# Averaging tile 1 by halves on two engines, and moving its sum of squares behind tile 3, at the start of a two-layer attention and feed-forward kernel

## The chip, the cores and the metric

The kernel runs on one core of one Trainium2 chip. The metric is the device time of one execution in microseconds (us). One execution per kernel was also recorded by the profiler; its span is about 1.8 us shorter than the timed value of the same execution. In the profile, PE is TensorE (matmul), PEld its weight loads, DVE is VectorE, ACT is ScalarE, POOL is GpSimd, SP is SyncE, and "SPq" or "ACTq" are the instructions with which SP and ACT issue DMAs.

## The reference, cut to what matters

```python
x = A_x                                       # 2048 tokens x 1024, bf16
x = x + _A_ref(_layernorm(x), A_wqkv, A_wo)   # sliding attention, 32 heads
x = x + _B_ref(_layernorm(x), B_w1, B_w3, B_w2)   # gated feed-forward, F = 3584
x = x + _A_ref(_layernorm(x), A_wqkv, A_wo)
x = x + _B_ref(_layernorm(x), B_w1, B_w3, B_w2)
return x
```

The layer norm subtracts the mean and divides by sqrt(var + 1e-5). The change touches only the very first layer norm and Q projection: the first 512 tokens, four tiles of 128 tokens each, called tiles 0 to 3.

## The kernel before

The kernel does not emit instructions in the order in which its text is written. It builds a list of operations with estimated durations, and a planner lays them out; the finished order is then emitted. On every engine, instructions run in that order.

```python
def place(self, n_banks=8, rate=330e3):
    # ... repeatedly takes the operation that can start first by the estimates:
    #     PE: the heads of three lanes (0 projections, 1 output projection, 2 transposes)
    #     other engines: smallest start, then class, then number
    ...
        if e in ("SP", "AQ"):                       # a DMA
            free[e] = t + op.dur                    # 0.45 us of the queue, for every DMA
            begin = max(pipe[e], t + 1.3)
            ...
    placed.sort(key=lambda o: (o.start, o.seq))
    return placed
# ... at the end of the kernel:
        for op in pr.place():
            op.emit(op)
```

The first Q projection (`q_first`) avoids waiting for a full layer norm of tiles 0 and 1. It only centres them (subtracts the mean), transposes the centred tiles on PE into `ce`, multiplies by Wq, and brings in 1/std later. The squares that give the std of tiles 0 and 1 run on ScalarE. Tiles 2 and 3 are fully normalized first (statistics, root, reciprocal, apply) and transposed on PE. The weights Wq come in eight row blocks, "row 0" to "row 7".

```python
dve(0.77, ... nc.vector.tensor_scalar(xn[2][:, 0:512], x_sb[0][:, 0:512], 1.0 / D, ..., accum_out=mean[:, 0:1]), ...)
act(0.82, ... nc.scalar.activation(xn[3][:, 0:512], x_sb[0][:, 512:1024], ..., accum_out=part[:, 0:1]), ...)
act(1.25, ... nc.scalar.activation(xn[3][:], x_sb[1][:], ..., accum_out=mean[:, 1:2]), ...)   # tile 1: all on ScalarE
for j in range(2):
    # centring of tile j in two halves on VectorE, then:
    transposed(xn[j], ..., ((0, 2, "DVE"), (2, 4, "DVE"), (4, 8, "ACT")) if j == 0 else ((0, 4, "DVE"), (4, 8, "ACT")))
...
for j in range(2, TPC):                       # tiles 2 and 3
    stats(j, ...); root(j, j + 1); apply(j); transposed(xn[j], ...)
for j in range(2):                            # squares of tiles 0 and 1, root, reciprocal, scaling
    act(1.25, ... ACTF.Square ..., accum_out=part[:, j:j + 1]), [..., ("ce", 1, KT - 1)], ...)
    ...
    dma(256, xnT[b][:, :, j * P:(j + 1) * P], xn[j][:], ..., transpose=True)     # for K and V
```

The K projection follows the Q projection; it needs all four tiles normalized and transposed in `xnT`, tiles 0 and 1 by DMA transpose. The loads of the next tokens wait for tile 1 to be normalized (`load_x(1, 0, 4, [("xn", 1)])`).

## Time and profile before

| | before |
|---|---|
| time, median of the first 3 runs | 1614.96 us (1614.86 to 1615.26) |
| span of the profiled run | 1613.1 us |
| PE busy | 1601.3 us |
| first matmul of the K projection | 21.49 us |

The page of the kernel before: busy time and share of the span with the number of instructions; PE's busy tenths in 40 slices; and, from the chain of work that ended last, the shares by engine.

```profile
PE 1601.3 (99%) x7463; PEld 762.7 (47%) x7610; DVE 1122.3 (70%) x1906; ACT 329.6 (20%) x526; POOL 5.3 (0%) x28
...
PE   9999999999999999999999999999999999999999
...
PE 99%; issue 1%; DMA 0%; ACT 0%; DVE 0%; ACTq 0%
```

The waits view of PE for the kernel before: who waited for whom, us in total, times, longest.

```profile
PE bank L285 <- PEq L757: 0.8, 1, 0.8
PE bank L430 <- DVE xn L472: 0.4, 1, 0.4
PE bank L521 <- DMA slot<-in_A_wqkv_dram: 0.2, 1, 0.2
```

So PE streams from about 7 us to the end, and nothing outside its queue is worth anything unless it makes PE wait. The timeline of the start, kernel before: start, duration, engine, line, operation, output from input, size, count, and in brackets the idle time before it and what ended it.

```profile
3.10 0.69 DVE L454 TENSOR_SCALAR_CACHE_REDUCE xn<-x 128x512 bf16<-128x512 bf16 x1 [2.10 <-DMA x<-in_A_x_dram]
...
5.37 1.06 ACT L460 ACTIVATE xn<-x 128x1024 bf16<-128x1024 bf16 x1 [1.35 <-DMA x<-in_A_x_dram]
...
6.33 0.19 ACT L460 ACTIVATION_READ_ACCUMULATOR xn<-x 128x1 f32 x1
...
6.55 0.62 DVE L472 TENSOR_SCALAR xn<-x,mean 128x512 bf16<-128x512 bf16 x2 [1.22 <-ACT xn L460]
...
6.96 0.66 PE L430 MATMUL bank<-ident,xn 128*128 128x128 bf16 x8 [0.39 <-DVE xn L472]
...
7.46 5.44 PE L521 MATMUL bank<-hT,slot 128*128 128x128 bf16 x64
...
14.51 7.15 PE L535 MATMUL bank<-xnT,slot 128*128 128x256 bf16 x64
...
21.49 8.80 PE L347 MATMUL bank<-xnT,slot 128*128 128x512 bf16 x39
```

The last line is the start of the K projection; its length and count end with the view's window. Tile 1's average (5.37 to 6.52) stands between its landing and its centring at 6.55, and PE waits 0.39 us for it. This wait is what the change is after.

### The profile page before, as it was taken

The page shows a single profiled execution, that of the slowest core. Times are in us where ns is not written, and L with a number is a line of the kernel's source. Part 1 is how long each engine was busy: PE and PEld are TensorE (multiplying, and loading weights), DVE is VectorE, ACT ScalarE, POOL GpSimd, SP SyncE. Part 2 cuts the span into 40 slices and gives each one's busy share as a digit, 9 for nine tenths or more (in the row PEclk, how much of TensorE's full clock was granted, in tenths as well). Part 3 has the DMA queues.
Part 4 walks back from the last instruction along what each step waited for, and adds up shares of the span by engine and source line. Part 5 has one row for each costly group of instructions (what it writes and reads, how often), then busy time and mean ns, then how long its engine had stood idle before and what let it go on. Part 6 is the DMA issues. An engine that isn't in the chain of part 4 may idle for free.

```text
span 1613.1 us, 19082 instructions
## 1 busy us (share of the span) xinstructions
PE 1601.3 (99%) x7463; PEld 762.7 (47%) x7610; DVE 1122.3 (70%) x1906; ACT 329.6 (20%) x526; POOL 5.3 (0%) x28
## 2 busy tenths in 40 slices
PE   9999999999999999999999999999999999999999
PEld 7555544444444444444444444444444444444444
DVE  5899888988889888898898729884299831211211
ACT  5423322021201222113311032110321101101110
POOL 1000000000000000000000000000000000000000
PEclk9999999999999999999999999999999999999999
DMA  9834755495548764858545487365873464454451
GB/s 321 228 105 151 221 166 171 127 227 158 171 141 253 194 186 137 216 164 251 176 131 163 157 248 228 121 176 174 254 220 118 160 179 156 144 177 149 156 167 42
DMA packets 350649, 285.80 MB, mean 177 GB/s; under 512 B 72288, under 2 KB 344928, under 8 KB 350560
## 3 DMA queue, kind: packets, MB, share of 16 engines
q1 hardware_dynamic: 350128, 283.94, 58.8%
q8 instruction: 59, 0.97, 0.2%
q10 hardware_dynamic: 432, 0.66, 0.1%
q14 instruction: 30, 0.25, 0.1%
HBM read 238.94 MB, written 29.36 MB: 166 GB/s over the span
## 4 chain that ended last, share of the span: by engine, by line
PE 99%; issue 1%; DMA 0%; ACT 0%; DVE 0%; ACTq 0%
PE bank L347 98%; PE bank L535 0%; PE bank L521 0%; DMA x<-in_A_x_dram 0%; PE bank L430 0%; ACT L281 0%; DVE xn L472 0%; ACT xn L460 0%; DVE x L700 0%; ACTq L460 0%
## 5 line engine op out<-in xcount | busy, mean ns | idle before, releaser
L347 PE MATMUL bank<-xnT,slot 128*128 128x512 bf16 x4955 | 1088.7, 379 | 5.3
L347 PEld LDWEIGHTS <-slot 128*128 128x128 bf16 x5056 | 518.2, 102 | 572.9
L347 PE MATMUL bank<-slot,hT 128*128 128x512 bf16 (+2 forms) x1812 | 387.3, 372 | 1.9
L670 DVE TENSOR_TENSOR hT<-sg,bank 128x512 bf16<-128x512 bf16 x224 | 153.4, 685 | 214.4 <-PE bank L347 194.9
L265 DVE TENSOR_TENSOR scr<-scr 128x1024 bf16<-128x1024 bf16 (+3 forms) x576 | 293.4, 539 | 2.0
L347 PEld LDWEIGHTS <-hT 128*128 128x128 bf16 x1848 | 178.5, 98 | 208.7
L668 ACT ACTIVATE sg<-bank 128x512 bf16<-128x512 f32 x224 | 133.7, 597 | 660.5 <-PE bank L347 608.8
L265 DVE TENSOR_TENSOR scr<-qT,kT 128x2048 bf16<-128x2048 bf16 x128 | 154.1, 1219 | 73.3 <-DMA kT<-qkv_d 71.0
L405 ACT CAST sgt<-bank 128x512 bf16<-128x512 f32 x184 | 107.3, 585 | 315.2 <-PE bank L347 300.3
L265 DVE TENSOR_TENSOR scr<-pA,vT 128x2048 bf16<-128x2048 bf16 x128 | 152.5, 1220 | 0.3
L700 DVE TENSOR_TENSOR x<-x,bank 128x512 bf16<-128x512 bf16 (+1 forms) x66 | 43.9, 670 | 121.5 <-PE bank L347 121.4
L347 PE MATMUL bank<-wo,oT 128*128 128x512 bf16 x502 | 112.6, 379 | 0.6
L313 DVE BATCH_NORM_STATS2 st<-x 128x6 f32<-128x512 bf16 x124 | 81.8, 681 | 11.9 <-DMA x<-in_A_x_dram 11.4
L347 PEld LDWEIGHTS <-oT 128*128 128x128 bf16 x512 | 50.1, 98 | 60.3
L645 DVE TENSOR_TENSOR x<-x,bank 128x512 bf16<-128x512 bf16 x64 | 43.9, 687 | 37.0 <-PE bank L347 35.8
L320 ACT ACTIVATE sd<-mv,epst 128x4 f32<-128x4 f32 (+1 forms) x17 | 5.1, 297 | 172.4 <-DVE mv L316 172.1
L628 DVE STREAM_TRANSPOSE pA<-pB 128x2048 bf16<-128x2048 bf16 x16 | 37.0, 2310 | 0.5
L605 DVE STREAM_TRANSPOSE pB<-pA 128x2048 bf16<-128x2048 bf16 x16 | 37.0, 2310 | 0.5
L668 ACT ACT_TABLE_LOAD x20 | 25.7, 1283 | 56.2 <-PE bank L347 56.0
L265 DVE TENSOR_TENSOR pA<-scr 128x256 bf16<-128x256 bf16 x128 | 35.9, 286 | 0.4
L265 DVE TENSOR_TENSOR oT<-scr 128x256 bf16<-128x256 bf16 x128 | 33.9, 288 | 0.1
L327 DVE TENSOR_SCALAR xn<-x,mv,rstd 128x1024 bf16<-128x1024 bf16 x62 | 30.7, 541 | 3.5 <-DMA xnT<-xn 3.4
(61 smaller groups left out, 209.0 us busy)
## 6 DMA issues: line engine op xcount, KB each, us to landing
slot<-in_B_w_dram SPq DMA_DIRECT2D x160, 1024.0 KB, 5.9
slot<-in_A_wqkv_dram SPq DMA_DIRECT2D x28, 1024.0 KB, 5.1
qkv_d<-sgt SPq DMA_DIRECT2D x92, 256.0 KB, 3.3
qT<-qkv_d SPq DMA_DIRECT2D x16, 512.0 KB, 5.7
slot<-in_B_w_dram SPq DMA_DIRECT2D x16, 512.0 KB, 5.7
kT<-qkv_d SPq DMA_DIRECT2D x14, 544.0 KB, 6.7
vT<-qkv_d SPq DMA_DIRECT2D x14, 544.0 KB, 4.9
out_dram<-x SPq DMA_DIRECT2D x31, 128.0 KB, 4.3
```

The lines of the kernel that those rows point to most:

```text
L265: return lambda _: nc.vector.tensor_tensor(o, a, b, op=op)
L313: dve(0.67, lambda _, hh=hh: nc.vector.bn_stats(st[q][:, j, hh, :], x_sb[n][:, hh * 512:(hh + 1) * 512]), [("x", n, hh)] + list(after), [( ...
L320: act(0.3, lambda _: nc.scalar.activation(sd[q][:, j0:j1], mv[q][:, j0:j1, 1], ACTF.Sqrt, bias=epst[:]), [("mv", q, j) for j in range(j0, ...
L327: dve(0.5, lambda _: nc.vector.tensor_scalar(xn[j][:], x_sb[n][:], mv[q][:, j, 0:1], rstd[q][:, j:j + 1], op0=ALU.subtract, op1=ALU.mult), ...
L347: nc.tensor.matmul(bank[a.bank][:, 0:ncol], lhsT=w, rhs=r, start=first and i == 0, stop=last and i == n - 1)
L405: evac(act, 0.59, lambda _, a=a, i=i, m=m: nc.scalar.copy(sgt[i][:, m % 2, :], bank[a.bank][:]), op, [], [("sgt", i, m % 2)], a)
L605: dve(2.31, lambda _: nc.vector.transpose(psmT[:].rearrange("p c d -> p (c d)"), psm[:].rearrange("p w s -> p (w s)")), allA, ["pB"])
L628: dve(2.31, lambda _: nc.vector.transpose(At[:].rearrange("p w s -> p (w s)"), AeT[:].rearrange("p c d -> p (c d)")), ["pB"], allA)
L645: evac(dve, t1(512), lambda _, xs=xs, a=a: nc.vector.tensor_tensor(xs, xs, bank[a.bank][:], op=ALU.add), op, [("x", n, hh)], [("x", n, hh) ...
L668: evac(act, 0.6, lambda _, i=i, a=ag: nc.scalar.activation(sg[i][:], bank[a.bank][:], ACTF.Silu), og, [], [("sg", i)], ag, table="silu")
L670: evac(dve, t1(512), lambda _, i=i, a=au, f=f: nc.vector.tensor_tensor(hT[:, f, :], sg[i][:], bank[a.bank][:], op=ALU.mult), ou, [("sg", i ...
L700: evac(dve, t1(cn), lambda _, xs=xs, a=a, cn=cn: nc.vector.tensor_tensor(xs, xs, bank[a.bank][:, 0:cn], op=ALU.add), op, [("x", n, hh)], [ ...
```

## The change

Tile 1 is averaged like tile 0: its left half on VectorE, its right half on ScalarE at the same time. Its centring takes the two partial means as two scalars, and its transposes are evacuated in three pieces. ScalarE's square of tile 1 moves behind the evacuation of tile 3's transposes, so that it stands in nobody's way.

```diff
-        act(1.25, lambda _: nc.scalar.activation(xn[3][:], x_sb[1][:], ACTF.Copy, scale=1.0 / D,
-                                                 accum_out=mean[:, 1:2]), [("x", 1, 0), ("x", 1, 1)], ...)
         for j in range(2):
+            dve(0.77, lambda _, j=j: nc.vector.tensor_scalar(xn[2][:, 0:512], x_sb[j][:, 0:512], ...,
+                                                             accum_out=mean[:, j:j + 1]),
+                [("x", j, 0)] + [("ce", 0, 2)] * j, [("xn", 2), ("mean", j)], -9)
+            act(0.82, lambda _, j=j: nc.scalar.activation(xn[3][:, 0:512], x_sb[j][:, 512:1024], ...,
+                                                          accum_out=part[:, j:j + 1]), ...)
 ...         # centring: mean and part as two scalars for both tiles
-                       ((0, 2, "DVE"), (2, 4, "DVE"), (4, 8, "ACT")) if j == 0 else ((0, 4, "DVE"), (4, 8, "ACT")))
+                       ((0, 2, "DVE"), (2, 4, "DVE"), (4, 8, "ACT")))
 ...         # the square:
-                [("x", j, 0), ("x", j, 1), ("mean", j)] + [("ce", 1, KT - 1)],
+                [("x", j, 0), ("x", j, 1), ("mean", j), ("xnT", b, 3, 1) if j else ("ce", 1, KT - 1)],
```

The loop also takes in tile 0's two averaging instructions, which stay as they were; their removed lines are left out here.

More of the change, by code (lines that the diff above doesn't have):

```diff
@@ L453, in q_first @@
         ce = hT[:, 8:16, :]
-        dve(0.77, lambda _: nc.vector.tensor_scalar(xn[2][:, 0:512], x_sb[0][:, 0:512], 1.0 / D, 0.0, op0=ALU.mult,
-                                                    op1=ALU.add, accum_out=mean[:, 0:1]),
-            [("x", 0, 0)], [("xn", 2), ("mean", 0)], -9)
-        act(0.82, lambda _: nc.scalar.activation(xn[3][:, 0:512], x_sb[0][:, 512:1024], ACTF.Copy, scale=1.0 / D,
-                                                 accum_out=part[:, 0:1]), [("x", 0, 1)], [("xn", 3), ("part", 0)], -9)
@@ L459, in q_first @@
-        rows[2](6, queue="AQ", after=[("part", 0)])
-        act(1.25, lambda _: nc.scalar.activation(xn[3][:], x_sb[1][:], ACTF.Copy, scale=1.0 / D,
-                                                 accum_out=mean[:, 1:2]), [("x", 1, 0), ("x", 1, 1)],
-            [("xn", 3), ("mean", 1)], -9)
-        for j in range(2):
-            for h in range(2):
-                c0 = 512 * h
-                if j == 0:
-                    dve(0.31, lambda _, c0=c0: nc.vector.tensor_scalar(
-                        xn[0][:, c0:c0 + 512], x_sb[0][:, c0:c0 + 512], mean[:, 0:1], part[:, 0:1], op0=ALU.subtract,
-                        op1=ALU.subtract), [("x", 0, 0), ("x", 0, 1), ("mean", 0), ("part", 0)],
-                        [("xn", 0), ("xn", 0, h)], -9)
-                else:
-                    dve(0.31, lambda _, c0=c0: nc.vector.tensor_scalar(
-                        xn[1][:, c0:c0 + 512], x_sb[1][:, c0:c0 + 512], mean[:, 1:2], None, op0=ALU.subtract),
-                        [("x", 1, 0), ("x", 1, 1), ("mean", 1)], [("xn", 1), ("xn", 1, h)], -9)
+        for j in range(2):
+            dve(0.77, lambda _, j=j: nc.vector.tensor_scalar(xn[2][:, 0:512], x_sb[j][:, 0:512], 1.0 / D, 0.0,
+                                                             op0=ALU.mult, op1=ALU.add, accum_out=mean[:, j:j + 1]),
+                [("x", j, 0)] + [("ce", 0, 2)] * j, [("xn", 2), ("mean", j)], -9)
+            act(0.82, lambda _, j=j: nc.scalar.activation(xn[3][:, 0:512], x_sb[j][:, 512:1024], ACTF.Copy,
+                                                          scale=1.0 / D, accum_out=part[:, j:j + 1]),
+                [("x", j, 1)], [("xn", 3), ("part", j)], -9)
+            if j == 0:
+                rows[2](6, queue="AQ", after=[("part", 0)])
+            for h in range(2):
+                dve(0.31, lambda _, j=j, c0=512 * h: nc.vector.tensor_scalar(
+                    xn[j][:, c0:c0 + 512], x_sb[j][:, c0:c0 + 512], mean[:, j:j + 1], part[:, j:j + 1],
+                    op0=ALU.subtract, op1=ALU.subtract), [("x", j, 0), ("x", j, 1), ("mean", j), ("part", j)],
+                    [("xn", j), ("xn", j, h)], -9)
@@ L475, in q_first @@
             transposed(xn[j], [("xn", j, h) for h in range(2)], ce[:, :, j * P:(j + 1) * P],
                        [("ce", j, k) for k in range(KT)],
-                       ((0, 2, "DVE"), (2, 4, "DVE"), (4, 8, "ACT")) if j == 0 else ((0, 4, "DVE"), (4, 8, "ACT")))
-        dve(0.16, lambda _: nc.vector.tensor_tensor(mean[:, 0:1], mean[:, 0:1], part[:, 0:1], op=ALU.add),
-            [("mean", 0), ("part", 0), ("ce", 1, 0)], [("mean", 0)], -9)
+                       ((0, 2, "DVE"), (2, 4, "DVE"), (4, 8, "ACT")))
@@ L480, in q_first @@
+        dve(0.16, lambda _: nc.vector.tensor_tensor(mean[:], mean[:], part[:], op=ALU.add),
+            [("mean", j) for j in range(2)] + [("part", j) for j in range(2)] + [("ce", 1, 0)],
+            [("mean", j) for j in range(2)], -9)
         for j in range(2, TPC):
```

## The prediction

> **What bounds the kernel.** TensorE. The page gives PE 1601.3 of 1613.1 us busy (99%), and the chain that ended last is 99% PE. From about 7 us to the end PE streams; the waits view of PE finds only three waits: 0.8 us at the start, 0.4 us for the centred tile 1, and 0.2 us for a weight row. The change touches only the first 22 us.
>
> **The stretch before, from the timeline.** Tile 1's data lets ScalarE start at 5.37. Its full-width average takes 5.37 to 6.52; VectorE idles 1.22 us, then centres from 6.55; the transposes of tile 1 start at 6.96. After that PE runs without a gap: matmuls from 7.46, transposes of tiles 2 and 3, the second group at 14.51, the K projection at 21.49.
>
> **Costs.** Removed: one 1024-wide ACT average (1.15 us). Added: a 512-wide half on VectorE (0.69 + 0.08, tile 0's durations) and one on ScalarE (0.63 + 0.19, overlapping to 0.72). The Trainium skill, "ScalarE: Activation LUTs", section "What ACT_TABLE_LOAD costs", gives 186 ns + 0.833 ns per element with immediates, 613 and 1039 ns; the trace shows 629 and 1057, so it agrees. Both halves end near 6.10, not 6.52: 0.42 us sooner. The centring with two scalars costs 0.41 per half instead of 0.35, which gives 0.06 back. The extra DVE copy (2 x 0.29 instead of 0.42) hides behind PE's matmuls. Net: transposes of tile 1 and everything behind them 0.3 to 0.35 us sooner. Weight row 5 (landing near 10.6) and tile 3's centring (12.86) are close behind PE and may take 0.1 of it.
>
> **The moved square.** Tile 1's square (1.23 us) now starts after ACT's last evacuation of tile 3, about 14.1 instead of 9.28. Then root (possibly behind one 0.59 us evacuation), reciprocal, scaling 0.53: normalized tile 1 is ready near 16.5 to 17.1 instead of 14.5. Tiles 2 and 3 gain nothing: their roots waited for VectorE's statistics, not for ACT. Tile 1's DMA transpose then issues some 2.5 us later. Before, it landed at about 19.9 (issue 14.9, 5.0 us to landing, held up behind the K weights); issued at 17, with the 3.1 to 5.0 us that other transposes took, it lands at 20.1 to 22. The K projection needs it at about 21.15. So there is some 40% chance of a new PE stall there, a few tenths to 1 us.
>
> **Prediction.** 0.3 us won, a quarter of a microsecond expected back: 1614.8 us, eight in ten within 1614.0 to 1616.2. Chances: faster by over 2% 0.003, within 2% 0.994, slower by over 2% 0.003.
>
> **What would show it.** Right: in the timeline the centring of tile 1 starts near 6.13, PE's transposes of tile 1 near 6.6, the second group near 14.2; the PE waits view shows the wait for the centring shrunk to under 0.15. If the K projection's first matmul starts near 21.15, the gain reaches the end; if the PE waits name the transposed tile (xnT) near 21, the move of the square ate it. Wrong: PE's second group still at 14.5.
>
> **What would make it wrong.** The kernel orders its instructions by a planner with estimated durations; a different order in the first 20 us or later, on the DMA queue above all, can add or remove small PE gaps. A stall at the K projection over 1.5 us; runs before spread by 0.4 us.

## The result

| | before | changed |
|---|---|---|
| time, median of 5 runs each | 1615.13 us (1614.86 to 1615.52) | 1615.94 us (1615.88 to 1616.3) |
| span of the profiled run | 1613.1 us | 1614.4 us |
| K projection's first matmul | 21.49 us | 21.89 us |
| PE wait near 188 us | none | 0.84 us |

The ratio is 1.0006 (95% interval 0.9992 to 1.0019). Ratios here are the mean time of one kernel's runs over that of the other's of the same rounds, so they are not quite the ratio of the quoted medians. The two sets of five runs do not overlap, so the loss of 0.8 us is small but seen. The measured time lies inside the predicted range; the gain that the prediction expected does not show.

The page of the changed kernel: busy time, then the chain's shares by engine.

```profile
PE 1602.1 (99%) x7463; PEld 763.0 (47%) x7610; DVE 1121.3 (69%) x1909; ACT 328.4 (20%) x525; POOL 4.9 (0%) x28
...
PE 98%; DVE 1%; issue 1%; DMA 0%; SPq 0%; ACT 0%
```

The waits view of PE, changed kernel.

```profile
PE bank L347 <- DVE scr L265: 0.8, 1, 0.8
PE bank L285 <- PEq L751: 0.8, 1, 0.8
PE bank L515 <- DMA slot<-in_A_wqkv_dram: 0.2, 1, 0.2
```

The timeline of the start, changed kernel.

```profile
3.63 0.69 DVE L455 TENSOR_SCALAR_CACHE_REDUCE xn<-x 128x512 bf16<-128x512 bf16 x1 [2.62 <-DMA x<-in_A_x_dram]
...
5.34 0.63 ACT L458 ACTIVATE xn<-x 128x512 bf16<-128x512 bf16 x1 [0.69 <-DMA x<-in_A_x_dram]
...
5.58 0.51 DVE L435 COPY hT<-bank 128x256 bf16<-128x256 bf16 x2 [0.16 <-PE bank L430]
...
6.00 0.68 DVE L455 TENSOR_SCALAR_CACHE_REDUCE xn<-x 128x512 bf16<-128x512 bf16 x1
...
6.80 0.74 DVE L464 TENSOR_SCALAR xn<-x,mean,part 128x512 bf16<-128x512 bf16 x2
...
7.20 0.62 PE L515 MATMUL bank<-hT,slot 128*128 128x128 bf16 x8 [0.20 <-DMA slot<-in_A_wqkv_dram]
...
7.65 0.61 PE L430 MATMUL bank<-ident,xn 128*128 128x128 bf16 x8
...
14.91 7.15 PE L529 MATMUL bank<-xnT,slot 128*128 128x256 bf16 x64
...
21.89 4.48 PE L347 MATMUL bank<-xnT,slot 128*128 128x512 bf16 x19
```

Two things are new. VectorE's half of tile 1 starts at 6.00, not when the data lands (5.34), because VectorE is still with tile 0's evacuations until 6.09. And PE does the matmuls of weight row 2 (7.20, waiting for the row) before tile 1's transposes (7.65); in the kernel before, the transposes came first. The PE wait for the centring is indeed gone from the waits view, but row 2's matmuls now fill that time, and PE waits 0.20 us for the row before them.

The K projection starts 0.4 us later in this pair of profiles; the experiments below show that profiles with one and the same start order differ by as much. The larger loss is far from the edited lines. PE's timeline between 165 and 190 us, kernel before; `wo` is the output projection of the second attention half, and what follows it are projections (`xnT`).

```profile
164.81 1.89 PE L347 MATMUL bank<-xnT,slot 128*128 128x512 bf16 x8
166.53 7.07 PE L347 MATMUL bank<-wo,oT 128*128 128x512 bf16 x31
173.44 16.78 PE L347 MATMUL bank<-xnT,slot 128*128 128x512 bf16 x76
```

The same view of the changed kernel.

```profile
164.78 4.05 PE L347 MATMUL bank<-xnT,slot 128*128 128x512 bf16 x18
168.66 7.07 PE L347 MATMUL bank<-wo,oT 128*128 128x512 bf16 x31
175.57 12.25 PE L347 MATMUL bank<-xnT,slot 128*128 128x512 bf16 x55
188.66 1.67 PE L347 MATMUL bank<-xnT,slot 128*128 128x512 bf16 x7 [0.84 <-DVE scr L265]
```

The output projection comes 2.13 us later: 0.4 us from the start, and one more group of 8 matmuls (1.73 us) ahead of it. Its result goes through residual addition, layer norm and DMA transposes into the first feed-forward matmul, the one that now waits at 188.66. The DMA queue of SP there, kernel before (the third line is the fourth transpose):

```profile
178.95 4.04 SPq L259 DMA_TRANSPOSE xnT<-xn  x3
183.09 0.54 SPq L261 DMA_DIRECT2D qkv_d<-sgt  x1
183.72 1.29 SPq L259 DMA_TRANSPOSE xnT<-xn  x1
```

The same view of the changed kernel.

```profile
180.62 1.27 SPq L259 DMA_TRANSPOSE xnT<-xn  x1
181.98 0.53 SPq L261 DMA_DIRECT2D qkv_d<-sgt  x1
182.60 4.04 SPq L259 DMA_TRANSPOSE xnT<-xn  x3
```

The last of the four transposes is issued at 183.72 before and at 185.4 in the changed kernel; each took 3.1 to 3.3 us to land. That gives about 186.9 and 188.6 (estimates, issue plus 3.2). PE wanted the data at 187.82 in the changed kernel. The wait is named after VectorE's score work (`scr`), which ended nearby; which of the two PE waits for was tested below.

### The profile page after: what moved, and what is told of

The parts are those of the page before. It is cut to its first block, busy times and chain, and to the rows that moved or that the text cites. A ratio compares the mean times of both kernels' runs of the same rounds, so it can differ in the third digit from the quotient of the medians.

```text
span 1614.4 us, 19077 instructions
## 1 busy us (share of the span) xinstructions
PE 1602.1 (99%) x7463; PEld 763.0 (47%) x7610; DVE 1121.3 (69%) x1909; ACT 328.4 (20%) x525; POOL 4.9 (0%) x28
## 4 chain that ended last, share of the span: by engine, by line
PE 98%; DVE 1%; issue 1%; DMA 0%; SPq 0%; ACT 0%
PE bank L347 97%; DVE scr L265 1%; PE bank L529 0%; PE bank L515 0%; DMA slot<-in_A_wqkv_dram 0%; DVE xn L327 0%; SPq L261 0%; PE bank L430 0%; DVE pA L265 0%; DVE x L639 0%; DVE st L313 0%; DVE hT L435 0%; ACT sd L320 0%; DVE x L694 0%; DVE rstd L322 0%
## 5 line engine op out<-in xcount | busy, mean ns | idle before, releaser
L662 ACT ACT_TABLE_LOAD x19 | 24.4, 1283 | 50.3 <-PE bank L347 50.1
L320 ACT ACTIVATE sd<-mv,epst 128x4 f32<-128x4 f32 (+1 forms) x17 | 5.1, 298 | 136.5 <-DVE mv L316 136.4
```

What stands on the lines that cost most here:

```text
L320: act(0.3, lambda _: nc.scalar.activation(sd[q][:, j0:j1], mv[q][:, j0:j1, 1], ACTF.Sqrt, bias=epst[:]), [("mv", q, j) for j in range(j0, ...
L662: evac(act, 0.6, lambda _, i=i, a=ag: nc.scalar.activation(sg[i][:], bank[a.bank][:], ACTF.Silu), og, [], [("sg", i)], ag, table="silu")
```

## The experiments

**Order theory:** the loss comes from the order of instructions that the planner chose, in the middle of the program above all. **Rivals:** the halves themselves are slower; or the differences at the start are noise of landings; or VectorE's score work causes the wait near 188 us.

All twelve runs gave correct results. "Before" is the median of the kernel before in the same rounds. K start is the K projection's first matmul, and wait is PE's wait near 188 us; both are from the one profiled execution. The median of `before_again` is of two runs, the others are of five.

| run | median us | before us | K start | wait | span |
|---|---|---|---|---|---|
| first result (changed) | 1615.94 | 1615.13 | 21.89 | 0.84 | 1614.4 |
| after_again | 1615.94 | 1614.99 | 21.89 | 1.01 | 1614.5 |
| square_only | 1615.98 | 1614.99 | 21.70 | 0.77 | 1614.1 |
| halves_only | 1615.75 | 1614.99 | 22.32 | none | 1614.0 |
| halves_old_plan | 1615.15 | 1614.99 | 21.75 | none | 1613.4 |
| before_again | 1615.13 | 1615.18 | 21.68 | none | 1613.3 |
| after_wo_first | 1615.91 | 1615.18 | 21.47 | 0.98 | 1614.1 |
| after_store_late | 1615.30 | 1615.18 | 21.66 | 0.17 | 1613.5 |
| after_transpose_first | 1616.01 | 1615.18 | 21.72 | 0.9 | 1614.2 |
| after_wo_root_first | 1615.30 | 1615.09 | 21.58 | 0.24 | 1613.4 |
| after_all_moves | 1614.97 | 1615.09 | 21.87 | none | 1613.3 |
| quarter_old_plan | 1614.99 | 1615.09 | 21.76 | none | 1613.4 |
| quarter_rows_swapped | 1614.93 | 1615.11 | 21.32 | none | 1613.0 |

Span minus K start minus wait is 1591.6 or 1591.7 us in every row (1591.4 in one), and 1591.6 in the first profile of before. So two numbers explain the differences of spans to 0.1 us, and to 0.2 us in `after_all_moves`, where the rest was not traced: when the K projection starts, and how long PE waits near 188 us.

### The changed kernel again

The kernel was run without an edit.

> The changed kernel once more, to see what of its profile repeats. Order theory (the loss comes from the order of instructions, which the planner laid differently): the same two losses, K projection's first matmul 0.3 to 0.5 us later than the 21.49 of before, and a PE wait of 0.7 to 1.0 us near 188 us; 0.6 to 1.0 us slower than before. Noise theory (tile 0's data landed 0.5 us late by chance, 3.63 instead of 3.10, and the delay ran on through VectorE): with tile 0 landing near 3.1, the K projection starts at 21.2 to 21.5 and the start's loss is gone.

Tile 0 landed earlier this time (VectorE began at 3.37, not 3.63), and yet the K projection began at 21.89 again, now with a wait for a weight row at 11.38. By the expectations this speaks for the order theory, but tile 0 did not land near 3.1, so the noise theory was not put to its test here. The wait near 188 us repeated, with another name on it:

```profile
PE bank L347 <- DMA xnT<-xn: 1.0, 1, 1.0
```

The same wait is named after VectorE in one profile and after the transposes in the next. A releaser is inferred from which event came last by the record; two events this close can trade places.

### Only the moved square

```diff
 # kernel before, one line
-                [("x", j, 0), ("x", j, 1), ("mean", j)] + [("ce", 1, KT - 1)],
+                [("x", j, 0), ("x", j, 1), ("mean", j), ("xnT", b, 3, 1) if j else ("ce", 1, KT - 1)],
```

> The kernel before with only the square of tile 1 moved behind tile 3's evacuation, planned anew. Order theory: the first 21 us as before (K at 21.5), but the output projection's matmuls lie one group of 8 matmuls later in PE's order than in before, so normalized tokens of the first feed-forward stage land too late: a PE wait of 0.6 to 1.1 us near 187 us, time +0.6 to +1.0 us against before. Rival (the mid stall comes from the halves): no such wait, time within 0.2 us of before.

PE's timeline between 165 and 190 us, this run:

```profile
168.47 7.07 PE L347 MATMUL bank<-wo,oT 128*128 128x512 bf16 x32
175.37 12.25 PE L347 MATMUL bank<-xnT,slot 128*128 128x512 bf16 x56
188.39 1.89 PE L347 MATMUL bank<-xnT,slot 128*128 128x512 bf16 x8 [0.77 <-DVE scr L265]
```

The moved square alone brings the later output projection and the wait, and the whole loss (+1.0 us by medians; one of its five runs took 1618.92). The rival that the halves cause the wait falls.

What lies between the two is read from the traces, not tested link by link. The later square makes tile 1 normalized late (17.25 us in this run, 14.50 before), and the loads of the next tokens wait for that (first one issued at 18.56 instead of 18.00, with stores now mixed in). The first finished attention output on VectorE came at 89.86 instead of 87.27. By the planner's own times, which are no measurement, the transposed tokens for the first feed-forward stage land 1.31 us before PE needs them in the order of before, and 0.20 us in this run's order. The planner counts 0.45 us of queue for a transpose where the trace shows 1.28, so a planned slack of 0.2 us is soon used up. It is no sharp limit: the plan of the next run left 0.3 us, and no wait shows there.

### Only the halves

```diff
 # changed kernel, one line: the square back at its old place
-                ... ("mean", j), ("xnT", b, 3, 1) if j else ("ce", 1, KT - 1)],
+                ... ("mean", j), ("ce", 1, KT - 1)],
```

> The change without the move of the square (square of tile 1 at its old place). Order theory: tile 1 transposed behind weight row 2 as in the changed kernel (+0.4 us), and in addition tile 3's transposes behind the last weight row in PE's order with nothing to do while it is evacuated, a PE wait of 0.7 to 1.1 us near 14 to 15 us; the planned slack near 188 us is only 0.3 us, so some wait there too (0 to 0.7). Sum +1.2 to +2.2 us against before. Rival (the halves are worth 0.3 us and only the moved square loses): within 0.5 us of before.

This lost 0.76 us by medians, less than the order theory expected and more than its rival, and all of it at the start (K start 22.32): a PE wait of 0.4 us at 15.34 for tile 3's evacuation, because tile 3's transposes now stood behind the last weight row with nothing after them to do, and tile 1's transposes behind row 2. PE's timeline, this run:

```profile
15.34 7.15 PE L529 MATMUL bank<-xnT,slot 128*128 128x256 bf16 x64 [0.41 <-DVE xnT L435]
```

Near 188 us there was no wait. So the two halves of the change do not add up: moving the square removes the wait at 15 us that the new averaging brought in the planner's order, and brings the one at 188 us.

### The halves in the order of before

The kernel before, its operations and its plan untouched, with only the emitted instructions replaced:

```diff
-        act(1.25, ... nc.scalar.activation(xn[3][:], x_sb[1][:], ..., accum_out=mean[:, 1:2]), ...)
+        act(1.25, ... nc.scalar.activation(xn[3][:, 0:512], x_sb[1][:, 512:1024], ..., accum_out=part[:, 1:2]), ...)
+        def centre1(c0):                       # emitted where tile 1's centring was
+            if c0 == 0:
+                nc.vector.tensor_scalar(xn[2][:, 0:512], x_sb[1][:, 0:512], ..., accum_out=mean[:, 1:2])
+            nc.vector.tensor_scalar(xn[1][:, c0:c0 + 512], ..., mean[:, 1:2], part[:, 1:2], subtract, subtract)
```

> The kernel before with its order of instructions kept, only the average of tile 1 done by halves: the VectorE half is emitted right in front of tile 1's centring, ScalarE's instruction covers half the width. Order theory: the gain that the prediction hoped for appears, centring of tile 1 near 6.2, transposes near 6.65, K projection near 21.2, no wait near 187 us, time -0.2 to -0.35 us against before. Rival (the halves themselves are no faster, since VectorE gets to its half only after tile 0's two evacuations): centring at 6.5 to 6.9, K projection at 21.5 or later, time 0 to +0.3 us.

The timeline of the start, this run:

```profile
5.80 0.68 DVE L465 TENSOR_SCALAR_CACHE_REDUCE xn<-x 128x512 bf16<-128x512 bf16 x1
...
6.59 0.73 DVE L467 TENSOR_SCALAR xn<-x,mean,part 128x512 bf16<-128x512 bf16 x2
```

The order theory's hope of a gain falls here; the rival holds: VectorE gets to its half only at 5.80, and the centring starts at 6.59, no sooner than the 6.55 of before. In this run tile 1 landed late (ScalarE began at 5.61), but VectorE's half, the later of the two, followed straight on its evacuations. (Counted from ScalarE's start the centring came after 0.98 us here, against 1.18 us in the first profile of before; with tile 1 landing at 5.02, in `after_transpose_first` below, the halves took until 6.66, which is 1.64 us.) The time is +0.16 us by medians. There is no wait near 188 us, since the order is that of before.

### The kernel before again

The kernel was run without an edit.

> The kernel before, profiled a second time, to see how far its own start varies. Order theory: the K projection's first matmul stays at 21.4 to 21.6 as in the first profile. Noise theory [...]: tile 0's data at 3.2 to 3.6 instead of 3.10, the warm-up's last matmul still slow, and the K projection at 21.6 to 21.8, as in the run that kept its start and moved only the square (21.70).

The noise theory's expectation held (tile 0 at 3.33, K start 21.68). The centring began at 6.20 this time, since tile 1 landed at 5.02. That is 0.35 us sooner than in the first profile, as much as the change was expected to win. Yet the K projection began 0.19 us later. The reason stands on PE's line of the timeline:

```profile
11.15 1.92 PE L521 MATMUL bank<-hT,slot 128*128 128x256 bf16 x16 [0.32 <-DMA slot<-in_A_wqkv_dram]
```

PE was early and waited for weight row 5. From that row on, PE has 10.5 us of matmuls and transposes to do before the K projection (21.68 - 11.15). In the first profile row 5 had landed at about 10.6 (issue 6.30, 4.3 us to landing), here at about 11.1 (issue 6.19, 4.9 us).

PE's line for tile 1's transposes in this run names no wait for the centring:

```profile
6.68 0.61 PE L430 MATMUL bank<-ident,xn 128*128 128x128 bf16 x8
```

Nor does the waits view of this run, or that of `square_only`, which kept the old averaging (the 0.3 us there is for tile 0's). So the wait of 0.39 us that the change was after stood in only one of three profiles with that averaging. And no loss at the start is shown: the five profiles with the start order of the changed kernel have K starts of 21.47 to 21.89 (mean 21.70), the three with the averaging and PE's order of before 21.49 to 21.70 (mean 21.62).

### Moving single instructions in the changed kernel's finished order

The planner's result is edited, and nothing else moves: `plan = pr.place()`, then an operation is taken out of the list and put in elsewhere. The edits are shown shortened, with some names changed.

First, the group of 8 matmuls that stands in front of the output projection near 167 us goes behind it (with its evacuation):

```diff
+        late = [group] + [o for o in plan if group in o.deps and o.eng == "ACT"]
+        # taken out, and put back behind the fourth group of the output projection
```

> The changed kernel with one move in PE's finished order: the K/V group of 8 matmuls that stands in front of the first output projection near 167 us is issued behind its four groups, as in the kernel before. Nothing else moves. Order theory: the residual additions, and with them the transposes, come 1.7 us sooner, and the PE wait near 188 us (0.8 to 1.0) is gone; 0.7 to 1.0 us faster than the changed kernel, so within 0.2 us of before plus what the start lost. Rival (VectorE's score work, which the chain of waits names, is the limit): the wait stays.

The output projection moved to 166.51, and the wait stayed at 0.98 us. The gain of 0.7 to 1.0 us did not come, and the wait stayed as the rival had said; taken alone, this run would speak for VectorE's score work. ScalarE's timeline there shows another reason (`L320` is the root of the feed-forward stage's layer norm):

```profile
177.12 0.59 ACT L405 CAST sgt<-bank 128x512 bf16<-128x512 f32 x1 [1.15 <-PE bank L347]
177.73 1.28 ACT L320 ACT_TABLE_LOAD   x1
179.02 0.30 ACT L320 ACTIVATE sd<-mv,epst 128x4 f32<-128x4 f32 x1
```

In ScalarE's order the root stands behind an evacuation whose matmuls end only at about 177.1; in the kernel before it stands ahead of it, at 177.31. So the early result on PE was worth nothing here, because ScalarE's queue was laid out for a late one. So the move was repeated with the root put ahead of that evacuation:

```diff
+        # in addition: the evacuation (and its store) ahead of the root goes behind the root
```

> The changed kernel with the output projection moved forward on PE as in the run before, and on ScalarE the root of the feed-forward stage (with its table load) put ahead of the evacuation that kept it waiting there. If the order on PE and ScalarE together causes the wait near 188 us, reciprocal near 177.7 instead of 179.4 to 179.8, transposes issued from about 178.9, no PE wait, time 0.8 to 1.0 us below the changed kernel (0 to 0.2 us above before). If the wait has another cause, it stays at 0.8 to 1.0.

The normalized tokens came at 178.0 instead of 180.05, the first transpose was issued at 178.65, and the wait shrank to 0.24 us. It did not vanish, because the store between the first and the second transpose now had to wait for its own data, until 181.30, and held the three transposes behind it in the queue. The median fell to 1615.30, though one of the five runs took 1617.09.

Second, alone in the changed kernel, that store goes behind the fourth transpose:

```diff
+        plan.remove(late_st)
+        plan.insert(plan.index(t3) + 1, late_st)      # t3: the fourth transpose
```

> The changed kernel with one move in the DMA queue's order: the store that stands between the first and second DMA transpose near 182 us is issued behind the fourth. If the wait near 188 us is for the fourth transpose's landing, it shrinks by the store's 0.6 us, from 0.8 to 1.0 to 0.2 to 0.4, and the time falls by as much. If it is for VectorE's score work, it stays at 0.8 to 1.0.

The DMA queue of SP, this run:

```profile
180.39 5.41 SPq L259 DMA_TRANSPOSE xnT<-xn  x4
```

And the waits view of PE:

```profile
PE bank L347 <- DMA xnT<-xn: 0.2, 1, 0.2
```

The wait fell to 0.17 us and the time to 1615.30, so 0.64 us less than the changed kernel by medians (of other rounds; in this run's own rounds the two other moves took 1615.91 and 1616.01). This shows what PE waits for: the landing of the fourth transpose. VectorE's score work was not touched.

Third, tile 1's transposes go ahead of weight row 2, as in the kernel before:

```diff
+        plan.remove(row2)
+        plan.insert(plan.index(tr1[-1]) + 1, row2)    # tr1: tile 1's transposes
```

> The changed kernel with one move in PE's order at the start: the matmuls of weight row 2 for tile 0 come behind tile 1's transposes, as in the kernel before. If that order is what the start lost, transposes of tile 1 at 6.9 to 7.2 instead of 7.26 to 7.65, K projection 0.2 to 0.4 us sooner (21.5 to 21.7), time down as much. If the weight rows' landing or tile 2 and 3 limit the start, the K projection stays at 21.8 to 21.9. The wait near 188 us stays at 0.8 to 1.2 in either case.

The transposes began at 7.13, after a wait of 0.16 us for the centring that is back with this order, and the K projection at 21.72, inside the spread of the runs that kept the changed order (21.47 to 21.89); the time did not fall (1616.01). So this order is not shown to cost anything by itself.

All four moves together:

> The changed kernel with all four moves: output projection, root, late store, and tile 1's transposes ahead of weight row 2. No PE wait near 188 us. If the change itself is worth something at the start, this beats before by 0.1 to 0.3 us; if the start is set by landings [...], it equals before within 0.2 us, with the K projection at 21.5 to 21.8.

There is no wait near 188 us, and the median is 1614.97 against 1615.09 of before, with the K projection at 21.87, just outside what was expected. So new orders alone take the whole loss away; the change itself is worth nothing that five runs can show.

### Why an earlier centring does not help

The order of before, with VectorE's share of tile 1 cut to a quarter so that both shares end together:

```diff
-  nc.scalar.activation(xn[3][:, 0:512], x_sb[1][:, 512:1024], ...)   nc.vector.tensor_scalar(xn[2][:, 0:512], x_sb[1][:, 0:512], ...)
+  nc.scalar.activation(xn[3][:, 0:768], x_sb[1][:, 256:1024], ...)   nc.vector.tensor_scalar(xn[2][:, 0:256], x_sb[1][:, 0:256], ...)
```

> Order of before, tile 1's average split unevenly: VectorE, which is late, takes 256 columns, ScalarE 768. If VectorE's late half is what ate the predicted gain, tile 1's centring starts at 6.2 to 6.4 when its data lands at 5.0 to 5.4 (6.59 with equal halves), and the transposes at 6.65 to 6.85. If that is what holds PE, the K projection comes at 21.4 to 21.6 and the time falls 0.1 to 0.3 us below before; if weight rows and later tiles hold PE behind it, the K projection stays at 21.6 to 21.8 and the time equals before within 0.15 us.

The timeline of the start, this run:

```profile
6.14 0.74 DVE L467 TENSOR_SCALAR xn<-x,mean,part 128x512 bf16<-128x512 bf16 x2
...
6.61 0.72 PE L430 MATMUL bank<-ident,xn 128*128 128x128 bf16 x8
...
11.22 1.92 PE L527 MATMUL bank<-hT,slot 128*128 128x256 bf16 x16 [0.29 <-DMA slot<-in_A_wqkv_dram]
```

Here are the predicted centring (6.13) and the predicted transposes (6.6), almost to the digit, and they buy nothing: PE waits 0.29 us for row 5 at 11.22, and the K projection comes at 21.76. Nor are they the work of the new averaging: tile 1 landed at 5.00 here, and in `before_again`, where it landed at 5.02, the old averaging gave 6.20 and 6.68.

The last run takes row 6, which comes early on the other queue, ahead of row 5:

```diff
-  [(k, 0, 2) for k in range(3, KT)]
+  [(k, 0, 2) for k in (3, 4, 6, 5, 7)]
```

> The uneven split in the order of before, and TensorE takes weight row 6 (loaded on the other queue, there early) ahead of row 5, for which it waited 0.29 us at 11.22 in the run before. If row 5's landing (11.1 to 11.3 in most profiles) is what holds the start, that wait is gone, tile 2's transposes come at 12.7 to 12.8 instead of 12.97 (not earlier, since tile 2 is normalized only at 12.7, behind tile 3's landing), the K projection at 21.5 to 21.6, time 0.1 to 0.3 us below before. If not, the K projection stays at 21.7 or later and the time equals before.

The wait for the row was gone, tile 2's transposes came at 12.42, and the K projection at 21.32, the earliest of all profiles. Both came earlier than expected. In this run tile 3 also landed early, and the warm-up was one of three short ones (see the open points), so the swap is not shown to be the cause. The times say less: median 1614.93 against 1615.11, with overlapping ranges (1614.76 to 1615.31 against 1614.86 to 1615.25). No version was shown to beat the kernel before.

## Why the prediction was right or wrong, point by point

- **"What bounds the kernel: TensorE."** Right. The differences of spans are the K projection's start plus one PE wait, to 0.2 us.
- **"Both halves end near 6.10, not 6.52."** Wrong; this is the first step that failed. It let VectorE's half start at the landing, 5.37. In the seven profiles with the changed kernel's start it began at 5.57 to 6.00, in its turn behind tile 0's two evacuations, and ended at about 6.7 in the first. The estimate rested on one trace in which tile 0 happened to land earliest (VectorE began at 3.10; in all other profiles at 3.23 to 3.63) and VectorE was free again at 5.34. Counted from ScalarE's start on tile 1, the old averaging began its centring after 1.18 us in all three profiles that have it; the equal halves in the changed order took 0.77 to 1.64 us, and longer than 1.18 in seven of eight profiles. So in most profiles the change made the centring later. ScalarE's half took what it should: 0.63 us for 512 columns.
- **"Net: transposes of tile 1 and everything behind them 0.3 to 0.35 us sooner."** Wrong, and for two more reasons. The wait to be won, 0.39 us, was in one of three profiles only. And even where the centring did come at 6.14, PE then waited for row 5: the prediction named it as "close behind PE" and gave it 0.1 us, and in that run it took 0.29 us.
- **"The centring with two scalars costs 0.41 per half instead of 0.35."** Right: 0.74 us for the pair against 0.62.
- **The moved square: a 40% chance of a new PE stall at the K projection near 21 us.** It did not occur; tile 1's transpose was issued at 17.47 and PE started the K projection without a wait. That the moved square costs PE something was right (`square_only`), but it was paid 167 us later, in an order that the planner laid.
- **"A different order in the first 20 us or later, on the DMA queue above all, can add or remove small PE gaps."** This caveat is what happened, at 0.8 to 1.0 us. It was listed as a risk and not put into the sum.
- **The total.** 1615.94 lies in 1614.0 to 1616.2, and "within 2%" held. The centre, 1614.8, was right about neither term: a gain of 0.3 that did not come, and a wait of 0.84 us that was not in the sum. That the range held is luck: the stall that it made room for, at 21 us, did not occur, and another of like size did.
- **Open.** Why the K projection starts at 21.5 in some runs and at 21.9 in others is shown only in part: row 5's landing (10.6 to 11.2 where it was read) and tile 0's landing vary between runs, and so does the length of PE's ten warm-up matmuls. These took 3.79 to 3.85 us in three profiles, which have the three earliest K starts (`quarter_rows_swapped` 21.32, `after_wo_first` 21.47, the first of before 21.49), and 4.01 to 4.43 us in the other eleven (21.58 and later). That goes together, but no run tested it. How these share the 0.4 us was not separated, nor was each link between the later tile 1 and the later attention tested.

## What to carry to other kernels

Before you cost a shortened wait, list everything that PE will meet next, with its landing time, and count only the smallest slack; and take landing times from several traces when the expected gain is a few tenths of a microsecond; look also whether the wait itself is there in a second profile. In a kernel whose order is planned from estimates, compare the order of instructions of both versions first: here the edited lines gained nothing that was measured, and a moved square on ScalarE put a 0.8 us wait 167 us later. Test such a cause by moving single instructions in the finished order, on all engines that the chain passes through, not on one.

## What the Trainium skill lacked or had wrong

- "TensorE: Matmul & The Clock Gate", Part 1, says that the array starts throttled and that the point of release varies by about 500 ns from run to run. The durations here fit that, and it matters at this scale: of the ten warm-up matmuls none was shorter than 586 ns in the changed kernel's profile, while the shortest of the kernel before took 379 ns. (The granted clock that the profile lists reads 1.00 from the start, so only the durations show it.) The lines are those of the warm-up matmuls (count, then least, median and largest duration in ns), first the kernel before:

```profile
L285 PE MATMUL bank<-const-bfloat16-1.0 x10: 379/631/631, 0.8 to 4.2; 128*128 128x512 bf16 x10
```

  and the changed kernel:

```profile
L285 PE MATMUL bank<-const-bfloat16-1.0 x10: 586/634/634, 0.8 to 4.6; 128*128 128x512 bf16 x10
```

  In the repeat of before, the first real transposes waited for the warm-up until 4.99 us instead of starting at 4.53. The page advises against fitting a count; it could add that a gain of 0.3 us at a kernel's start cannot be judged from one profile.
- "DMA: Bandwidth & Descriptors", section "Latency and other measured facts", gives a rate for DMA transposes (261 GB/s, 350 to 400 GB/s if contiguous) but no page gives, for trn2, how long one of this size holds its queue. Here a transpose of 256 KB near 180 us took 1.28 us of SP's queue and landed 3.1 to 3.3 us after issue, and taking out the store between two of them let the fourth issue 0.7 us sooner after the first. The one at 13.8 in the changed kernel held 2.02 us and took 5.5 us to land.
- "ScalarE: Activation LUTs", section "What ACT_TABLE_LOAD costs", gives 1283 ns for a load plus about 1380 ns of drain, 2.66 us in all, for each switch. The load took 1.28 us here, but no drain shows around it: the evacuation at 177.12 took 0.59, the load began at 177.73, and the root at 179.02.
